# Another program order for a fused polysketch-attention and feed-forward kernel

## Chip, cores and metric

The kernel runs on one core of a Trainium2 chip. The metric is the device time of one execution in microseconds (us); the figure for a kernel is the median over its runs. The core has five engines that run side by side, each through its own instruction queue and strictly in the order in which the instructions stand there: TensorE (PE, matrix products; its weight loads are shown apart as PEld), VectorE (DVE), ScalarE (ACT), GpSimd (POOL) and SyncE (SP, which here only issues DMA transfers). Matrix products write to PSUM; everything else lives in SBUF. Engines wait for one another through semaphores.

## What is computed

Two stages: attention with a quadratic feature map (4 batches, 4 heads, 1088 positions, head dimension 32, r = 8), whose output is laid out as 4352 tokens by 128 and goes through a multiplicative feed-forward network.

```python
def phi(x):                                       # attention, r = 8
    a = np.einsum('rd,bhsd->bhsr', S1, x)
    b = np.einsum('rd,bhsd->bhsr', S2, x)
    return np.einsum('bhsi,bhsj->bhsij', a, b).reshape(*x.shape[:-1], r * r)
q_p, k_p = (phi(q), phi(k))
kv = np.einsum('bhsf,bhsd->bhfd', k_p, v)
z = np.sum(k_p, axis=2)
num = np.einsum('bhsf,bhfd->bhsd', q_p, kv)
den = np.einsum('bhsf,bhf->bhs', q_p, z)[..., None] + 1e-06
attn_out = num / den
x = attn_out.transpose(0, 2, 1, 3).reshape(4352, 128)
a = x @ w1                                        # feed-forward: 128 -> 1024
b = x @ w2
h = a * b @ w3                                    # 1024 x 1024
out = h @ w_out                                   # 1024 -> 128
```

q, k and v are float32; the sketch matrices S1, S2 and the four weights arrive as float64 and are read as raw 64-bit words.

## The kernel before

The whole program is a set of some 950 named steps, each a few instructions, that the function `make_steps` defines, and one long string `ORDER` that names every step once. The entry function runs the steps in the order of the string and then chains the instructions of each engine, so that the place of a name in `ORDER` is the place of its instructions in its engine's queue. Nothing else schedules; buffers are handed out in that order too, and a step that takes a buffer waits until the earlier users of that buffer are done.

The names have two parts, the object and the step.

**Weights, `w0` to `w10`.** `w0` and `w1` hold halves of w1 and w2, `w2` holds w_out, `w3` to `w10` the eight row blocks of w3. Each is 1 MB of 64-bit words. `.load` issues the DMA (SP, L291 to L301; there are three buffers `raw`), `.c` and `.m` read the high and the low words (ACT, L184 and L321), `.j` and `.a` put them together (DVE, L332 and L337).

**Folds, `f0` to `f7`.** Because h is used only through w_out, the kernel computes w3 @ w_out once: `.t` transposes a block of w3 (DVE, L365), `.m` multiplies it with w_out (16 products on PE, L371), `.o` copies the result out (ACT, L375).

**Keys, `k0` to `k3` (one per batch).** `.load`, `.loadr`, `kh.load` and `v.load` are DMAs; k, v and kh have a single buffer each, so batch b + 1 can be loaded only when batch b's readers are done. `.max`, `.g`, `.lead`, `.rest` split k into an exact leading part and a rest (DVE); `.gram0` and up multiply k by itself (PE, L480, 144 small products for a batch), which leads through `.Gm`, `.Gt`, `.Ga`, `.Gb`, `.T0`, `.T1`, `.Ta`, `.Tb`, `.Ts`, `.N0`, `.N1`, `.Na`, `.Nb`, `.Nh`, `.Nf`, `.Nl` to the matrix with which a query's denominator is found. `.kT`, `.ab`, `.abt`, `.kp` form the key features, `.kv` (64 small products) and `.kvr` multiply them by v, `.kvm`, `.kzt`, `.kz` bring the result into the form the queries need. `kr0` and `kr1` do the same for the last 64 positions of two batches. For `k0` the feature product `.kp` runs on POOL (L503).

**Queries, `q0` to `q7` and `qr`** (512 tokens each, `qr` the 256 that remain). `.tr`, `.max`, `.l2`, `.l1`, `.rm` transpose and split (DVE and ACT), `.A0`, `.C0` are the small products with the sketch and with N (PE, L798 to L887), a dozen short DVE steps from `.sm` to `.rc` give the denominator, `.phi` the features, `.pt0`, `.pt1` and `.x` bring them through PE (L1008, L1053), `.xT` is the copy of the 128 x 512 block of x (ACT). `q0` has further steps `.A1`, `.C1`, `.xs`, `.xt` of the same kind.

**Feed-forward, `g0` to `g7` and `gr`,** over the same token blocks. For each of the eight column blocks c: `.ca` is x @ w1 (PE, L1087), `.cc` copies it out of PSUM (ACT, L1092), `.cb` is x @ w2 (PE, L1097), `.cm` multiplies the two (DVE, L1103, into one of 17 buffers `ab`), `.co` adds the product with the folded weights into the output (PE, L1109). `g0.1a` is thus the first product of column block 1 of token block 0. `.oT` transposes the output (DVE), `.st` stores it (SP, L1065). The products `.ca`, `.cb` and the folds share three PSUM buffers `h`. The two instructions of such a step take 0.86 us.

**Warm-up, `warm0` to `warm8`:** products of zeros (L176; 15, 5, 3, 1, 6, 15, 4, 2 and 5 of them) that nobody reads. `c.act` is a dummy copy that makes ACT load its function table.

A weight load and its product are called a pair below; the program has 2134 pairs on PE.

Of the kernel before, what the change touches and what calls it, by code (L numbers as in the profile page):

```python
# [30 lines left out]


ORDER = """
c.zeros v0.zero c.ident c.mask k0.zero k0.load0 k0.loadr k0.load1 s.load c.act q0.load v0.loadr w0.load
k0.max0 w1.load k0.max1 k0.nat1 kr0.load warm0 k0.tr1 k0.g0 k0.g1 k0.lead0 k0.kT1 k0.lead1 kh1.load k0.nat0
k0.rest0 s.words k0.rest1 warm1 k0.gram0 s.pair q0.tr s.split k0.gram1 q1.tr w0.c v0.load q0.max k0.tr0
k0.Gm s.T k0.Gt k0.kT0 w0.j k1.zero s.P k1.load q0.l2 s.blk k0.Ga s.blkh warm2 k0.ab1 k0.Gb q0.l1 s.Pp k1.loadr
q0.A0 k0.ab0 w2.load q0.rm k0.T0 k0.T1 k0.abc0 kr0.tr k0.abc1 k0.Ta k0.kp0 warm3 q0.C0 w1.c k1.kT1 q1.max w1.m
k0.Tb q0.sma q0.restT kr0.kT k0.Ts w0.m k0.kp1 warm4 k0.kv0 k1.max k0.N0 k0.N1 q0.sta w3.load k0.Na q0.sha
k0.Nh k0.Nb q0.sla kr1.load warm5 q0.A1 k0.Nl k0.Nf kr0.ab q0.sca k0.kv3 q0.smy kr0.abc q0.al k0.kv1 kr0.kp  # L40
q0.sty q0.C1 q0.phi w4.load q1.l2 k0.kv2 k0.kvr v1.zero q1.l1 q0.shy warm6 q0.pt0 k0.kvm q0.C1t q0.sly k0.kzt
q0.pt1 q0.pc0 q0.scy v1.load q0.p01 q1.A0 k0.kz q0.pc1 q0.p2 warm7 q0.x q1.rm q0.p12 w1.j w3.c q0.dn q0.de w2.c
q1.sm q1.C0 q0.rc q1.st q0.xs w0.a q0.xt q0.xT q1.sh w2.m k1.g w1.a warm8 g0.1a g0.1b w2.j g0.1c w5.load 
k1.lead g0.0a g0.1m kr1.tr g0.6a kr1.kT g0.0c k1.rest g0.0b w2.a kr1.ab g0.6b g0.6c w3.m g0.5a g0.0m g0.6m
g0.7a g0.5c w6.load q1.sl kr1.abc k1.kT0 g0.5b w3.j g0.7b g0.5m q1.load w4.c k1.gram0 w3.a g0.7c k1.ab w4.m
q1.sca q1.scy f0.t k1.gram1 w5.c w7.load k1.gram2 q1.al q1.p01 g0.2a q1.p2 k2.zero g0.7m q1.p12 kh2.load
g0.4a w4.j g0.2c q1.dn f0.m g0.4c w4.a w6.c k2.load q1.de k1.Gm f1.t v1.loadr w5.m g0.2b g0.4b q1.rc g0.2m f0.o
w10.load f1.m k1.Gt q1.bs q2.tr w6.m q1.phi g0.0o k1.abt f1.o w8.load q1.pt1 k1.Ga q2.max q1.pt0 w5.j
g0.3a q1.pc0 g0.4m q1.pc1 k2.loadr q1.x k1.kp1 g0.1o q1.xT w5.a q2.l2 g1.1a g0.3c k1.Gb g0.3b f2.t g1.1c q2.l1
k1.T0 k1.T1 g1.5a g0.3m f2.m k1.Ta g1.5c k1.kp0 w7.c w7.m w6.j g1.1b k1.Tb g1.6a w6.a f2.o w9.load k1.kv0  # L50
g1.1m k1.kv2 k1.kv3 k1.kv1 w8.c w7.j k1.kvr g0.2o f3.t g1.5b w7.a f3.m g1.6c k1.kvm k1.Ts g1.5m w8.j g1.6b
f3.o f4.t k1.N0 w9.c k1.N1 g1.4a g1.6m g1.4b k1.Na g1.4c k2.max f4.m g1.4m w8.m k1.Nb g1.0a k2.g w9.j f4.o
g1.0b k1.Nf q2.rm g1.0c w10.c k2.lead g0.3o k1.Nl k1.Nh g1.3a g1.0m k2.rest g1.2a g1.3c w9.m g0.4o q3.tr w8.a
k2.gram0 k2.gram1 k2.kT1 q2.C0 f5.t k2.kT0 k2.gram2 q3.max q2.A0 k2.ab k3.zero k3.loadr v2.zero w9.a kr1.kp
q3.l2 v2.load f5.m g1.2c q2.At q3.l1 q2.Ct q2.sm q3.rm g1.7a f5.o q2.st f6.t g1.3b w10.m g0.5o q2.sh w10.j
f6.m q2.sl g1.3m q2.sca q2.scy q2.al q3.A0 q2.p01 f6.o q3.C0 g1.7c w10.a g1.2b q2.p2 f7.t g1.7b q2.p12 q2.dn
f7.m k2.Gm q2.de q1.restT q2.rc q2.load q2.bs q3.At v2.loadr q3.Ct g0.6o kh3.load q2.phi f7.o g0.7o k2.abt
q2.pt0 k3.load g0.oT q2.pt1 g1.2m k1.kzt g1.0o g0.st k1.kz q2.pc0 q3.sm g1.7m q2.pc1 g1.2o k2.Gt q3.st g1.5o
q3.sh q3.sl q2.x k2.kp0 g1.3o q2.xT q3.sca k3.max g2.7a g2.1a k3.g k2.Ga q3.p01 k2.kp1 g2.7b g2.1c g2.7c g1.1o
q5.tr g1.6o q5.max q3.al k3.lead g1.4o q4.tr g1.7o k2.Gb g2.5a g2.7m q4.max g2.1b q3.scy k3.rest g2.5b k2.kv0  # L60
q3.p2 k3.gram0 g2.1m q3.p12 g2.5c k3.gram1 k3.kT0 g2.5m k2.kv3 k2.kv1 k2.kv2 g1.oT k2.kvr k3.gram2 v3.zero
v3.load k2.kvm q3.dn k2.T0 k2.T1 g2.2a k3.Gm k2.Ta g2.3a k2.Tb v3.loadr g2.2c k2.Ts q3.de q4.l2 g1.st q3.rc
k2.N0 q3.bs k2.N1 q3.phi g2.2b q4.l1 g2.3c g2.0a g2.2m k2.Na g2.3b g2.0c k2.Nb q3.pt1 k2.Nh k3.kT1 g2.0b g2.3m
q3.pt0 q4.rm g2.6a k2.Nf g2.0m g2.4b g2.6c k3.Gt k2.Nl q3.pc0 g2.4a q3.pc1 q3.x q4.A0 q3.xT q4.C0 g2.4c k3.ab
g2.0o k3.abt g2.4m g3.3a g2.6b g2.2o g2.6m k3.Ga g3.3b q4.At g3.3c q4.sm g2.5o q4.st q4.Ct g3.2b g3.3m q4.sh
g3.2a k3.kp0 k2.kzt g2.1o g3.2c q5.l2 g3.2m g3.4a k3.kp1 g2.4o g3.4c k2.kz q4.sl q5.l1 g3.4b q4.sca k3.Gb g3.6a
# [12 lines left out]
g5.5c q6.bs g5.6a g4.oT g5.6b g4.st g5.6c qr.xT g5.0o g5.6m q7.sm g5.5b q7.st g5.4a g5.5m q7.sh g5.4b g5.4c
q6.phi g5.5o q7.Ct g5.1a g5.4m q6.pt0 g5.3b q6.pc0 q6.pt1 g5.3a q6.pc1 g5.1c q6.x g5.3c g5.3m g5.1b q6.xT g5.6o  # L80
g5.1m q7.sl g5.4o q7.sca g5.1o g5.3o g6.1a g5.2o g6.1c g6.1b g6.4a g6.1m q7.scy g6.6a q7.al g6.4c q7.p01 g6.4b
g6.6c g5.7o g6.4m q7.p2 g6.6b g5.oT q7.p12 g6.0a g5.st g6.6m q7.dn g6.0b g6.0c g6.5a g6.0m g6.3a g6.5c g6.3b
g6.3c g6.5b g6.3m q7.de gr.2b g6.5m g6.0o q7.rc q7.bs g6.2a q7.phi gr.2a g6.2c g6.4o gr.2c gr.2m g6.6o g6.2b
gr.0a g6.2m q7.pt1 gr.0b gr.0c q7.pt0 gr.0m g6.7a q7.pc0 g6.7b g6.7c q7.pc1 q7.x g6.7m g6.5o q7.xT g7.1a g7.1b
g7.1c g7.0a g7.1m g6.2o g7.3a g6.3o g7.3c g7.0c g7.0b g6.1o g7.0m g6.7o g7.3b g6.oT g7.4a g6.st g7.3m g7.4b
g7.4c g7.2b g7.4m g7.2a g7.6a g7.2c g7.2m g7.0o g7.6c g7.2o g7.5a g7.1o g7.5c g7.6b g7.7a g7.6m g7.5b g7.7c
gr.5a g7.5m g7.7b gr.6a g7.7m g7.5o gr.6c gr.5c g7.3o gr.6b gr.5b g7.6o gr.5m gr.6m gr.4b gr.4a g7.4o gr.4c
gr.4m gr.1b gr.1a g7.7o gr.1c gr.1m gr.3a g7.oT gr.3b gr.3c gr.7a g7.st gr.3m gr.0o gr.7c gr.6o gr.2o gr.5o
gr.7b gr.3o gr.7m gr.1o gr.4o gr.7o gr.oc gr.ot gr.oT gr.st
"""  # L90


# [4 lines left out]
def make_steps(ctx, tc, q, k, v, S1, S2, moe_w1, moe_w2, moe_w3, moe_w_out, out):  # L97
    nc = tc.nc
    dve, act, pe, pool, sp = nc.vector, nc.scalar, nc.tensor, nc.gpsimd, nc.sync
# [398 lines left out]
    def kv(b):  # L498
        a = acc[b]
        f = {}  # L500
# [5 lines left out]
        if b == 0:  # L506
            for half in range(2):
# [22 lines left out]

                @step(f"k{b}.abc{half}")
# [609 lines left out]
    for g in range(8):  # L1141
        b, half = divmod(g, 2)
# [56 lines left out]
```

## Time and profile before

| what | value |
|---|---|
| time, median of 3 runs | 279.46 us (279.44 to 281.6) |
| span of the profiled execution, first to last instruction | 278.9 us |
| PE busy | 263.7 us, 95% of the span |
| DVE busy | 187.6 us, 67% |
| ACT busy | 97.1 us, 35% |
| POOL busy | 8.2 us, 3% |
| first feed-forward product `g0.1a` starts | 36.60 us |
| last product of `gr` ends | 274.06 us |

The profile shows one execution: busy time of each engine, the chain of work that ended last followed back from the end, groups of instructions by line, who waited for whom, and every engine's instructions in order of time. Times inside it count from the first instruction. The profiled span lies 0.56 us under the median.

### The profile page before, as it was taken

The page shows a single profiled execution, that of the slowest core. Times are in us where ns is not written, and L with a number is a line of the kernel's source. Part 1 is how long each engine was busy: PE and PEld are TensorE (multiplying, and loading weights), DVE is VectorE, ACT ScalarE, POOL GpSimd, SP SyncE. Part 2 cuts the span into 40 slices and gives each one's busy share as a digit, 9 for nine tenths or more (in the row PEclk, how much of TensorE's full clock was granted, in tenths as well). Part 3 has the DMA queues.
Part 4 walks back from the last instruction along what each step waited for, and adds up shares of the span by engine and source line. Part 5 has one row for each costly group of instructions (what it writes and reads, how often), then busy time and mean ns, then how long its engine had stood idle before and what let it go on. Part 6 is the DMA issues. An engine that isn't in the chain of part 4 may idle for free.

```text
span 278.9 us, 5282 instructions
## 1 busy us (share of the span) xinstructions
PE 263.7 (95%) x2134; PEld 149.7 (54%) x2134; DVE 187.6 (67%) x427; ACT 97.1 (35%) x167; POOL 8.2 (3%) x33
## 2 busy tenths in 40 slices
PE   7985999799998999979999999999999999999993
PEld 5874956455656763454544545445544446344572
DVE  4978699798999988976398855466773255231330
ACT  3552466636273213123231143163223221413121
POOL 2051000000001000000000000000000000000000
PEclk9998699999999999999999999999999999999999
DMA  7999969999800364040002200200020020002011
GB/s 201 329 250 217 211 130 213 237 235 213 166 1 6 79 170 105 0 112 10 2 0 81 38 2 0 38 2 0 2 39 0 1 40 0 0 5 33 0 20 39
DMA packets 32168, 22.50 MB, mean 81 GB/s; under 512 B 21392, under 2 KB 26640, under 8 KB 32144
## 3 DMA queue, kind: packets, MB, share of 16 engines
q1 hardware_dynamic: 31600, 21.64, 35.2%
q10 hardware_dynamic: 544, 0.52, 0.6%
q8 instruction: 17, 0.28, 0.5%
q14 instruction: 7, 0.06, 0.1%
HBM read 19.93 MB, written 2.23 MB: 79 GB/s over the span
## 4 chain that ended last, share of the span: by engine, by line
PE 85%; DMA 6%; SPq 2%; issue 2%; DVE 1%; ACT 1%; ACTq 0%; DVEq 0%
PE a_ps L1087 21%; PE b_ps L1097 21%; PE ps_o L1109 20%; PE ps_w3o L371 5%; DMA raw<-in_moe_w_dram 3%; PE ps_x L1053 3%; PE ps_ph L1008 3%; PE ps_c L798 3%; DMA k<-in_k_dram 3%; PE ps_g L480 2%; PE ps_kv L578 1%; PE ps_ab L553 1%; PE ps_xt L1027 1%; SPq L1065 1%; DMA out_dram<-oT 1%
## 5 line engine op out<-in xcount | busy, mean ns | idle before, releaser
L1103 DVE TENSOR_TENSOR ab<-ffa,b_ps 128x512 f32<-128x512 f32 (+1 forms) x72 | 46.8, 651 | 57.8 <-PE b_ps L1097 44.3
L1092 ACT COPY ffa<-a_ps 128x512 f32<-128x512 f32 (+1 forms) x72 | 39.7, 562 | 101.6 <-PE a_ps L1087 89.7
L1087 PE MATMUL a_ps<-xT,w 128*128 128x512 f32 (+1 forms) x144 | 69.1, 575 | 0.1
L1097 PE MATMUL b_ps<-xT,w 128*128 128x512 f32 (+1 forms) x144 | 68.8, 572 | 0.0
L1109 PE MATMUL ps_o<-ab,w3o 128*128 128x512 f32 (+1 forms) x144 | 67.4, 574 | 0.0
L1097 PEld LDWEIGHTS b_ps<-xT,w 128*128 128x128 f32 x144 | 26.4, 190 | 28.4 <-issue 25.2
L1109 PEld LDWEIGHTS ps_o<-ab,w3o 128*128 128x128 f32 x144 | 26.1, 190 | 26.2 <-issue 23.1
L1087 PEld LDWEIGHTS a_ps<-xT,w 128*128 128x128 f32 x144 | 25.9, 190 | 25.8 <-issue 20.7
L371 PEld LDWEIGHTS ps_w3o<-wo,w3T 128*128 128x128 f32 x128 | 15.5, 192 | 5.9 <-issue 5.0
L371 PE MATMUL ps_w3o<-wo,w3T 128*128 128x128 f32 x128 | 16.1, 277 | 1.7 <-issue 1.7
L184 ACT ACTIVATE cv_c<-raw 128x1024 f32<-128x1024 f32 x11 | 12.7, 1166 | 8.9 <-DMA raw<-in_moe_w_dram 8.9
L1014 ACT COPY pT<-ps_ph 128x512 f32<-128x512 f32 (+1 forms) x18 | 9.9, 566 | 10.9 <-PE ps_ph L1008 10.9
L321 ACT ACTIVATE cv_m<-raw 128x1024 int32<-128x1024 uint32 x11 | 12.7, 1156 | 0.0
L1008 PEld LDWEIGHTS ps_ph<-ident,ph 128*128 128x128 f32 x68 | 9.1, 151 | 6.6 <-issue 4.6
L176 PE MATMUL idle_ps<-zeros 128*128 128x256 bf16 x56 | 10.6, 340 | 1.7 <-DVE zeros L151 1.1
L480 PE MATMUL ps_g<-kk 128*32 128x64 f32 x288 | 10.4, 228 | 1.7 <-issue 1.7
L480 PE MATMUL ps_g<-k,kk 128*32 128x32 f32 x288 | 9.9, 197 | 1.3 <-issue 1.3
L1008 PE MATMUL ps_ph<-ident,ph 128*128 128x128 f32 x68 | 11.0, 290 | 0.0
L480 PEld LDWEIGHTS ps_g<-kk 128*32 128x32 f32 x288 | 8.8, 112 | 3.5 <-issue 2.1
L480 PEld LDWEIGHTS ps_g<-k,kk 128*32 128x32 f32 x288 | 9.2, 114 | 1.8 <-issue 1.8
L365 DVE STREAM_TRANSPOSE w3T<-w3c 128x1024 f32<-128x1024 f32 x8 | 9.8, 1230 | 0.0
L337 DVE CUSTOM_DVE_ANT_0 w3c<-w3c,cv_m 128x2048 uint16<-128x2048 uint16 x8 | 9.6, 1203 | 0.0
(196 smaller groups left out, 281.4 us busy)
## 6 DMA issues: line engine op xcount, KB each, us to landing
raw<-in_moe_w_dram SPq DMA_DIRECT2D x32, 256.0 KB, 7.8
qh<-in_q_dram SPq DMA_DIRECT2D x4, 544.0 KB, 4.2
raw<-in_moe_w_dram SPq DMA_DIRECT2D x4, 512.0 KB, 6.1
out_dram<-oT SPq DMA_DIRECT2D x32, 64.0 KB, 2.0
kh<-in_k_dram SPq DMA_DIRECT2D x12, 128.0 KB, 7.5
k<-in_k_dram SPq DMA_DIRECT2D x3, 512.0 KB, 7.5
v<-in_v_dram SPq DMA_DIRECT2D x12, 128.0 KB, 3.3
raw<-in_moe_w_out_dram SPq DMA_DIRECT2D x4, 256.0 KB, 9.2
```

The lines of the kernel that those rows point to most:

```text
L176: pe.matmul(t[:, :256], zeros[:, :128], zeros, start=True, stop=True)
L184: act.activation(dst, hi.bitcast(F32), ACT.Prelu, scale=2.0 ** -112, alpha=-2.0 ** 32)
L321: act.mul(shape(x["m"], 1, True), words(0).bitcast(U32), 2.0 ** -29)
L371: pe.matmul(t["o"], w3T[ko][:, c], wo[:, c], start=c == 0, stop=c == NC - 1)
L480: pe.matmul(o[h * D:(h + 1) * D], lhs, rhs, start=start, stop=stop, skip_group_check=True)
L1008: pe.transpose(t[:, j * 128:(j + 1) * 128], ph_cols(j, p), ident)
L1014: act.copy(s["pT"][:, p, :n], s["pp", p][:, :n])
L1087: pe.matmul(x["a"][:, :w], w_of(0, c), xT[g][:, c0:c0 + w], start=True, stop=True)
L1092: act.copy(x["s"][:, :w], x["a"][:, :w])
L1097: pe.matmul(x["b"][:, :w], w_of(1, c), xT[g][:, c0:c0 + w], start=True, stop=True)
L1103: dve.tensor_mul(ab_sb[g, c][:, c0:c0 + w], x["s"][:, :w], x["b"][:, :w])
L1109: pe.matmul(o_ps[g][:, :n], w3o[:, c], ab_sb.pop((g, c))[:, :n], start=c == 0, stop=c == NC - 1)
```

## The change

The string `ORDER` is replaced by another permutation of the same step names; every step and every instruction stays. A second edit goes with it: the dictionary that holds the transposed keys `kT` is indexed by batch and half in place of half alone, so that the steps `.kT` of one batch may stand ahead of readers of another. The three products of `warm2` now come last of all, after the final store, and `c.act` stands far down, so that ACT's table load goes with its first real copy, `k0.nat0`.

The diff, cut to the start of the string, the stretches around the key products of batches 1 to 3, and the end:

```diff
-c.zeros v0.zero c.ident c.mask k0.zero k0.load0 k0.loadr k0.load1 s.load c.act q0.load v0.loadr w0.load
-k0.max0 w1.load k0.max1 k0.nat1 kr0.load warm0 k0.tr1 k0.g0 k0.g1 k0.lead0 k0.kT1 k0.lead1 kh1.load k0.nat0
-k0.rest0 s.words k0.rest1 warm1 k0.gram0 s.pair q0.tr s.split k0.gram1 q1.tr w0.c v0.load q0.max k0.tr0
-k0.Gm s.T k0.Gt k0.kT0 w0.j k1.zero s.P k1.load q0.l2 s.blk k0.Ga s.blkh warm2 k0.ab1 k0.Gb q0.l1 s.Pp k1.loadr
-q0.A0 k0.ab0 w2.load q0.rm k0.T0 k0.T1 k0.abc0 kr0.tr k0.abc1 k0.Ta k0.kp0 warm3 q0.C0 w1.c k1.kT1 q1.max w1.m
-k0.Tb q0.sma q0.restT kr0.kT k0.Ts w0.m k0.kp1 warm4 k0.kv0 k1.max k0.N0 k0.N1 q0.sta w3.load k0.Na q0.sha
...
-q1.sm q1.C0 q0.rc q1.st q0.xs w0.a q0.xt q0.xT q1.sh w2.m k1.g w1.a warm8 g0.1a g0.1b w2.j g0.1c w5.load 
...
-g0.7a g0.5c w6.load q1.sl kr1.abc k1.kT0 g0.5b w3.j g0.7b g0.5m q1.load w4.c k1.gram0 w3.a g0.7c k1.ab w4.m
-q1.sca q1.scy f0.t k1.gram1 w5.c w7.load k1.gram2 q1.al q1.p01 g0.2a q1.p2 k2.zero g0.7m q1.p12 kh2.load
...
-k2.gram0 k2.gram1 k2.kT1 q2.C0 f5.t k2.kT0 k2.gram2 q3.max q2.A0 k2.ab k3.zero k3.loadr v2.zero w9.a kr1.kp
...
-q5.tr g1.6o q5.max q3.al k3.lead g1.4o q4.tr g1.7o k2.Gb g2.5a g2.7m q4.max g2.1b q3.scy k3.rest g2.5b k2.kv0
-q3.p2 k3.gram0 g2.1m q3.p12 g2.5c k3.gram1 k3.kT0 g2.5m k2.kv3 k2.kv1 k2.kv2 g1.oT k2.kvr k3.gram2 v3.zero
...
-gr.7b gr.3o gr.7m gr.1o gr.4o gr.7o gr.oc gr.ot gr.oT gr.st
+k0.zero c.zeros warm7 c.mask k0.loadr warm5 v0.zero k0.load0 k0.max0 c.ident k0.load1 s.load k0.nat0 k0.g0 k0.lead0
+k0.nat1 w0.load q0.load kr0.load k0.max1 s.words warm8 warm3 w0.c k0.tr0 k0.rest0 k0.tr1 k0.gram0 k0.g1 k0.lead1
+s.pair k0.rest1 k0.gram1 k1.zero s.split q0.tr k0.kT1 k0.kT0 s.T s.blkh q0.max s.P warm6 q0.l2 kr0.tr k0.Gm q1.tr
+k0.Gt s.blk k0.ab1 w1.load k1.loadr k0.Ga w0.j q0.l1 q0.A0 q0.rm s.Pp k0.Gb warm1 v0.loadr k0.ab0 k0.T0 q1.max
+k0.T1 w0.m k0.Ta k0.Tb q0.C0 k1.load k0.N0 k1.max q0.sma k0.Ts k0.N1 q0.sta k0.abc1 v0.load k0.kp1 k1.g kr0.kT
+k0.Na k0.abc0 k0.Nb k0.kp0 k0.kv0 k0.Nh q0.sha k0.kv3 k0.kv1 kr0.ab k0.Nf q0.A1 k0.Nl q0.sla q0.sca q0.smy w1.m
+q0.al q0.phi kr0.abc w3.load q0.sty k0.kv2 q0.shy q0.C1 q0.C1t kr0.kp warm0 q0.sly q0.pt0 k0.kvr k1.lead k0.kvm
+q0.scy q0.p01 q0.p2 q0.pt1 k0.kzt q1.l2 q1.l1 q1.A0 q1.sm q0.p12 q0.dn q0.pc0 q1.rm q0.de q0.pc1 k0.kz w3.c q0.x
+kh1.load k1.kT0 q0.rc q1.C0 w1.c w1.j q0.xs q1.st w0.a q0.xt w1.a q0.xT warm4 q1.sh g0.1a g0.1c k1.rest q1.sl
+kr1.load g0.0b g0.0a w3.m g0.0c w4.load w4.c kr1.tr w3.j g0.6a w2.load g0.1b k1.gram0 q1.sca k1.gram1 w3.a q1.scy
+g0.1m q1.al g0.0m kr1.kT k1.gram2 k1.kT1 q1.p01 q1.p2 g0.6b w2.m k1.Gm g0.6c q1.p12 q1.dn w4.m k1.Gt k2.zero g0.5a
...
+g1.0b g0.3o w8.a k2.rest g1.0m kh3.load w9.m w10.c k2.gram0 k2.gram1 w10.m q3.max k2.ab f5.t kr1.kp q2.sm w10.j
...
+q3.C0 q2.sca g1.3m q2.al f7.t q2.p01 q2.scy q2.p2 k2.gram2 k2.Gm k3.zero k3.loadr q2.p12 k2.abt q2.dn k3.load q3.At
...
+g2.2a k2.kv0 k2.kv3 q4.max q3.bs q3.phi k2.kv1 k2.kv2 k3.gram0 k2.kvr k2.kvm k3.gram1 k2.T0 k2.T1 g2.2c q4.l2 g2.3a
+g2.2m k2.Ta k2.Tb g2.3c q4.l1 k2.Ts g1.2o k2.N0 k2.N1 g2.6a g2.0a g2.3b g2.6c v3.zero k2.Na k2.Nf k2.Nh g2.3m k2.Nb
...
+k3.kT1 q3.load q4.A0 k3.gram2 g2.0m q4.C0 q4.At q4.sm q4.st g1.oT k3.ab g2.0o q4.Ct q4.sh g2.4m g3.2a q4.sl q5.l2
...
+gr.oc gr.ot gr.oT gr.st warm2
...
-                    kT[half] = sb("t2", [128, 512], name="kT")
-                    act.copy(kT[half], f["pt", half].rearrange("p j x -> p (j x)"))
+                    kT[b, half] = sb("t2", [128, 512], name="kT")
+                    act.copy(kT[b, half], f["pt", half].rearrange("p j x -> p (j x)"))
```

## The prediction

> **What bounds the kernel now.** First the page: how full the engines are, and where.
>
> ```profile
> PE 263.7 (95%) x2134; PEld 149.7 (54%) x2134; DVE 187.6 (67%) x427; ACT 97.1 (35%) x167; POOL 8.2 (3%) x33
> PE   7985999799998999979999999999999999999993
> DVE  4978699798999988976398855466773255231330
> PEclk9998699999999999999999999999999999999999
> DMA  7999969999800364040002200200020020002011
> q8 instruction: 17, 0.28, 0.5%
> ```
>
> PE is full from about slice 6 on, but for dips. VectorE is as full up to slice 17 (some 120 us) and half idle after, so it may bound the first part, never the second. The DMA engines are full up to 75 us. Next the chain of waits in order of time (start, length, what), as its head and its breaks:
>
> ```profile
> 14.23 7.41 DMA k<-in_k_dram
> 21.76 1.35 DVE k_g L140
> 31.22 2.46 PE ps_xt L1027 x16
> 36.60 1.12 PE a_ps L1087 x2
> ...
> 51.40 1.72 issue
> ...
> 87.41 1.25 issue
> ...
> 120.21 1.73 issue
> ```
>
> Up to 36.60 no feed-forward product can run: the chain goes through the load of `k1`, VectorE's `k1.max`, the denominator steps and `q0`. From 36.60 the chain is PE, but for three breaks in which PE waits for nothing that the profile shows. Last, cumulative windows (length; busy and count of PE, PEld, DVE, ACT, POOL; clock, DMA) up to those breaks:
>
> ```profile
> 0.00:51.41 51.41, 45.31 (x602) 34.22 (x602) 41.75 (x106) 26.34 (x41) 6.94 (x29) 0.93 0.96 224
> 0.00:87.30 87.30, 79.48 (x982) 55.46 (x983) 74.25 (x165) 44.39 (x67) 6.94 (x29) 0.96 0.86 192
> 0.00:120.20 120.20, 111.13 (x1363) 74.49 (x1364) 105.18 (x227) 52.05 (x82) 8.17 (x33) 0.97 0.71 160
> ```
>
> The breaks come after 602, 982 and 1363 pairs: 380 and 381 apart, three times 127. The instruction queue moved 17 blocks of 16 KB, one per 2134/17 = 126 pairs. I read the breaks as PE at the end of a block with the next not there.
>
> **Term 1, the start.** Before, `k1.load` was issued at 13.80, behind `kh1.load` and `v0.load`; it landed at 21.6, `k1.max` ran 21.76 to 23.1, `k0.Nh` ended at 24.16, `q0.xs` began at 33.72, `g0.1a` at 36.60. In the new order `k1.load` stands ahead of `kh1`, `v0` and `w3`. It still waits for the last reader of the single k buffer, `k0.gram1`. ACT's table load (1.28 us, before under the k load) now comes behind that load, so `k0.nat0` ends near 6.4 and the transposes of `k0.nat0` and `nat1` (1.5 us) stand ahead of the gram products (3.7 us): gram ends near 11.5, against 11.2 before. `k1.loadr` and `v0.loadr` (0.6 each) go first, so `k1.load` starts near 13.3. Landing: 2.0 us (shortest median of a bulk row, the stores) to 7.4 (its own row), that is 15.3 to 20.7. VectorE meanwhile: `s.split` to 10.5, `q0.tr` 0.6, `s.blkh` after PE's transposes at 12.2, then `q0.max`, `q1.tr`, `w0.j`, `q0.rm` (0.6 each), `s.Pp` 1.3, the `k0.G`, `Ta`, `Tb` steps: `k1.max` at 18.6 at the earliest. From there to `Nh` are 3.4 us of rows: 22.1 with the data early; with `k1` at 20.7, 23.8. `Nh` to `xs` was 9.56 us with 2.0 us of idle for `q0.x` (PE at clock 0.5 after a 2.72 us gap); the steps now listed there (`k1.lead`, `k1.kT0`, `q1.rm`, `w1.j` among them) sum to 9.2: `xs` 31.2 to 33.0; then `xs`, `xt`, `xT` 2.0 to 2.9. `g0.1a`: 33.2 to 35.9. Costs not seen before on this path: VectorE's `T_p` step took 1.74 us in place of 0.18 while POOL ran `kp`; that can now hit a step that matters, so 36.6 is the other end. I take 34.2, nearer the early end because `k1` no longer shares with `kh1`: **-2.4 us (-3.4 to 0).** The 56 warm-up products (0.12 to 0.23 us each) are redistributed in gaps; the last three run under the final store (2.1 us): 0.
>
> **Term 2, the breaks.** The 857th pair came at 85.10 and the 984th at 88.67; the 1238th at 118.44 and the 1365th at 121.95: 3.5 us for a block is what the fetch allows with DMA quiet. The 476th to 603rd took 6.8 us under full DMA (46.31 to 53.13). Now PE's work per block, from rows (0.86 us per feed-forward step, 1.78 a fold, 0.6 per 48 gram pairs, 0.22 per 16 kv pairs, 0.97 `C0`, 0.86 `k.ab`). Before, the three broken blocks hold 4.9, 2.1 and 1.7 us: `k1`'s gram with `k1.ab`; `k2`'s with `q2.C0`; `k2`'s kv with `k3`'s gram. All others hold 9.5 or more. In the new order `k1.ab` stands 9 products after the gram, `k2.gram2` and `k3.gram2` are split off from their batch, `q2.C0` comes four products ahead. The same boundaries then cut blocks of 11.5, 15.1, 13.3, 5.5, 6.4, 18.1, 10.7, 7.9 us and longer. None is under 3.5. At the price of full DMA two would break for 1.7 us together, but DMA is quiet after 75 us. **-4.7 us (-4.7 to -3.0; 0 if the reading is wrong).**
>
> [...]
>
> **Term 3, VectorE as the next bound.** What is late once PE comes earlier? From `g0.1a` on, PE's work is the same to 0.2 us (225.8 against 225.6 by rows; spent 237.5, so 4.7 in breaks and 7.2 in small turns between kinds). I sum VectorE's steps from `q0.xs` and PE's from `g0.1a` to each point where PE needs VectorE. Before, VectorE is at most 1.4 us behind PE's bare sum. In the new order it is behind from `k2.gram0` on, by 2.5 at `f6.m`, most at `k2.N0`: VectorE 82.5 us from the end of `xs` (32.9 when `g0.1a` is at 34.2), thus 115.4 bare; PE 78.4 bare and 3.9 of turns, 116.5. VectorE's idle time between 35 and 120 was 6.0 us:
>
> ```profile
> 50.00:55.00 5.00, 3.28 (x20) 2.37 (x19) 3.46 (x7) 3.61 (x6) 0.00 (x0) 1.00 1.05 242
> 80.00:85.00 5.00, 5.00 (x50) 2.21 (x52) 5.00 (x10) 3.28 (x4) 0.00 (x0) 1.00 0.00 2
> 85.00:90.00 5.00, 3.75 (x187) 3.25 (x174) 5.00 (x8) 1.49 (x3) 0.69 (x3) 1.00 0.03 7
> 100.00:105.00 5.00, 5.00 (x29) 3.45 (x28) 3.91 (x7) 1.15 (x4) 0.00 (x0) 1.00 0.94 254
> ```
>
> Its largest piece, 1.54 us, lies beside the break at 51.4. With half of the idle, 3.0, it reaches `k2.N0` at 118.5: **+2.0 us (0 with none, +5.0 with all).** The weights are not behind this: `w7` to `w10` are now loaded in a row; by the bytes ahead of them (213 GB/s) they land at about 60 to 79, VectorE wants them from 67 to 83. `w2` moves behind `w3`, `kh1`, `kr1`, `w4` and lands near 39; its ACT step stands ahead of `g0.6c` and can hold that copy by about 1 us, which the gram products on PE cover. After `k2.N0` VectorE has slack and the rest is PE: 147.4 and 3.2 of turns.
>
> **The end** is the same: the last output copy needs both PE's last product (274.06) and the store before it (274.14); `g7.st` now has 6 us of products behind `g7.7o` where it had 5. 4.84 us, 0.
>
> **Sum** against the execution's own 278.9: -2.4 - 4.7 + 2.0 + 0.2 = 274.0; the median lies 0.56 above: **274.6 us.**
>
> **Rivals.**
> - *VectorE keeps up* and the start is at its early end: -3.4 - 4.7 + 0.2 gives 271.6. For it: VectorE's idle lay partly beside PE's breaks. Against: VectorE stands at 5.00 of 5 us from 80 to 95.
> - *The gain ends in a wait for VectorE:* all 6.0 us of idle stay. `k2.N0` at 32.9 + 82.5 + 6.0 = 121.4, plus 150.6 + 4.84 + 0.56: 277.4, and 278.8 with a start gained by 1.0 only. No measurable change (one per cent, 2.8 us, is what a measurement tells from none).
> - *Slower, VectorE's in-order queue:* its steps up to `k2.N0` have no slack now, so each wait put on it by another order of copies and products is paid in full. With twice the idle, 12 us: 127.4, so 283.4. It turns slower than before from 8.1 us of idle on, and measurably from 10.9. For it: 98% busy leaves no room, and the new order has not been lived in by this engine; against: no wait that I could place by sums exceeds 3 us.
> - *The breaks are something else* and stay: 274.6 + 4.7 = 279.3, less VectorE's waits, which they would cover (2.0): 277.3. No change.
>
> **Numbers.** Forecast 0.50 (its own range 272.5 to 276.6), VectorE keeps up 0.15, gain ends in a wait 0.14, breaks stay 0.07, slower 0.14. Faster by over 1% (under 276.7): 0.65; within: 0.21; slower: 0.14. Range 270.8 to 280.5: the lower end takes in the early start with a little less turning, the upper both cases of no change and the beginning of the slow one.
>
> **What would show it.** `g0.1a` near 34 (33.2 to 36.6); `k1.max` without a wait for DMA over 2 us; no PE wait on "issue" over 1 us after it, 127 pairs never passing under 3.5 us; `k2.N0` near 118 with PE waiting for VectorE about 2 us in all between 70 and 118; the end of PE 151 us later. Wrong if `k2.N0` comes after 124, if breaks of 1.2 us or more appear at other multiples of 127 pairs, or if the stretch after 120 has PE gaps, for which I found no reason.

## The result and the profile after

| | before | changed |
|---|---|---|
| median (range, runs) | 279.46 us (277.37 to 283.24, 19) | 276.66 us (274.96 to 277.55, 19) |
| ratio | | 0.9893, 95% interval 0.9868 to 0.9918 |
| profiled execution: time, span | | 277.46, 275.7 us |
| `g0.1a` starts | 36.60 | 36.79 |
| `k2.N0` starts | 124.33 | 120.56 |
| last product of `gr` ends | 274.06 | 270.91 |

(The ratio leaves out the disturbed runs, which the medians and ranges include, so the two can differ a little.) The change is faster by 1.1%. That is 2.8 us where 4.9 were forecast: 276.66 us lies within the range of 270.8 to 280.5, and 0.06 us above the narrower 272.5 to 276.6 that the forecast gave itself. The page of the changed kernel, busy times and slices:

```profile
PE 266.5 (97%) x2134; PEld 150.8 (55%) x2134; DVE 189.2 (69%) x427; ACT 97.6 (35%) x167; POOL 8.3 (3%) x33
PE   7899999989999999999999999999999999999994
DVE  4888899998899999957988456666682534223130
PEclk9965899999999999999999999999999999999999
DMA  6989479999951075200410002001020002001020
q8 instruction: 17, 0.28, 0.5%
```

From the tenth slice on PE never drops under 9 until the last: the three dips are gone, with the same 17 blocks fetched. New is the 6 and 5 in PEclk, in the slices from 14 to 28 us. The chain of waits (start, length, what):

```profile
8.07 3.17 PE ps_g L478 x141
...
26.89 2.82 PE idle_ps L174 x15
29.71 0.44 PE ps_ph L1006 x4
30.14 0.29 PE ps_kv L583 x8
...
30.46 0.29 DVE kvm L589
...
34.50 0.68 DVE xs L1031
...
53.72 0.97 issue
...
58.82 1.27 PE ps_w3o L369 x9
```

The load of `k1` is no longer in it, nor is an "issue" of PE; the one at 53.72 lies between two steps of VectorE, with VectorE (`q1.phi`) and PE both busy beside it. In its place stand PE's small products and `warm0`, most of them at half clock, and behind them VectorE up to 58.8. The chain goes through VectorE again between 77.8 and 92.2 and between 113.3 and 118.7, but there PE waits for it only twice, 0.2 us each. By stages (length; busy and count of PE, PEld, DVE, ACT, POOL; clock, DMA share, GB/s):

```profile
5.20:15.40 10.20, 8.02 (x186) 6.84 (x186) 8.84 (x27) 6.74 (x11) 0.20 (x1) 1.00 0.83 258
15.40:29.10 13.70, 13.70 (x138) 11.81 (x135) 11.78 (x38) 3.82 (x8) 4.53 (x3) 0.50 1.02 248
29.10:36.79 7.69, 7.05 (x69) 6.24 (x67) 6.61 (x17) 4.01 (x6) 0.00 (x0) 1.00 0.46 108
36.79:120.56 83.77, 82.55 (x937) 48.56 (x937) 80.43 (x157) 39.32 (x61) 1.62 (x6) 1.00 0.65 146
35.00:60.00 25.00, 24.12 (x247) 13.84 (x247) 24.88 (x43) 16.27 (x23) 0.40 (x2) 1.00 0.93 215
```

The same view of the kernel before, around its own stretch of half clock:

```profile
22.40:25.80 3.40, 1.26 (x51) 1.20 (x54) 3.30 (x17) 0.21 (x1) 0.40 (x1) 1.00 1.12 216
25.80:32.60 6.80, 6.18 (x63) 5.34 (x56) 5.43 (x16) 3.74 (x6) 0.42 (x2) 0.50 1.07 209
```

So before, PE ran at half clock for 6.8 us, now for 13.7, and `g0.1a` starts no earlier. The gain came after it: to the end of PE 237.5 us before, 234.1 now. VectorE is busy 24.88 of the 25 us from 35 on. The changed kernel's 19 times lie in two groups that go with the mean clock listed with each run: ten of 276.66 to 277.55 us with a clock of 0.971 to 0.975 and nine of 274.96 to 276.14 with 0.978 to 0.990. In the profiled runs a mean clock of 0.974 went with 13.7 us at half speed (the changed kernel) and one of 0.986 with 6.8 (`e12_m_first` below).

### The profile page after: what moved, and what is told of

The parts are those of the page before. It is cut to its first block, busy times and chain, and to the rows that moved or that the text cites. A ratio compares the mean times of both kernels' runs of the same rounds, so it can differ in the third digit from the quotient of the medians.

```text
span 275.7 us, 5281 instructions
## 1 busy us (share of the span) xinstructions
PE 266.5 (97%) x2134; PEld 150.8 (55%) x2134; DVE 189.2 (69%) x427; ACT 97.6 (35%) x167; POOL 8.3 (3%) x33
## 4 chain that ended last, share of the span: by engine, by line
PE 78%; DVE 17%; issue 2%; DMA 1%; ACT 1%; ACTq 0%; DVEq 0%
PE ps_o L1107 20%; PE a_ps L1085 18%; PE b_ps L1095 18%; PE ps_w3o L369 3%; PE ps_x L1051 3%; DVE ab L1101 2%; PE ps_c L796 2%; PE ps_ph L1006 2%; DVE w3c L335 2%; DVE w3T L363 2%; PE ps_g L478 2%; PE ps_kv L576 1%; PE idle_ps L174 1%; DMA k<-in_k_dram 1%; DVE kp L501 1%
## 5 line engine op out<-in xcount | busy, mean ns | idle before, releaser
L1006 PEld LDWEIGHTS ps_ph<-ident,ph 128*128 128x128 f32 x68 | 8.2, 140 | 7.0 <-issue 5.1
L1006 PE MATMUL ps_ph<-ident,ph 128*128 128x128 f32 x68 | 10.1, 273 | 0.0
L478 PE MATMUL ps_g<-kk 128*32 128x64 f32 x288 | 9.2, 224 | 0.0
L995 DVE TENSOR_TENSOR ph<-s_al,s_bs 128x1024 f32<-128x1024 f32 (+1 forms) x8 | 9.1, 1136 | 0.1
L174 PEld LDWEIGHTS <-zeros 128*128 128x128 bf16 x56 | 6.6, 124 | 4.3 <-issue 1.2
```

The costliest lines, as they stand in the source:

```text
L174: pe.matmul(t[:, :256], zeros[:, :128], zeros, start=True, stop=True)
L478: pe.matmul(o[h * D:(h + 1) * D], lhs, rhs, start=start, stop=stop, skip_group_check=True)
L1006: pe.transpose(t[:, j * 128:(j + 1) * 128], ph_cols(j, p), ident)
```

## Experiments

Two theories of the breaks (instruction fetch or something else), two of the start (halves of the order are independent, or not), then the clock, VectorE and PE's gap. Zero products that nobody reads are added in some; nothing else is changed but the order, except where said.

**One half of the order alone.** `e1_start_before` has the old order of all steps up to `g0.1a` and the rest in the new order, `e2_start_after` the reverse; the few steps that this would drop (`k1.lead` and `k1.kT0` in the first) stand just ahead of `g0.1a`. The diff of the first against the changed kernel, cut to its first line:

```diff
-k0.zero c.zeros warm7 c.mask k0.loadr warm5 v0.zero k0.load0 k0.max0 c.ident k0.load1 s.load k0.nat0 k0.g0 k0.lead0
...
+c.zeros v0.zero c.ident c.mask k0.zero k0.load0 k0.loadr k0.load1 s.load c.act q0.load v0.loadr w0.load k0.max0
...
```

> Old order up to the first feed-forward product g0.1a, the new order for all that follows. My theory: the start is worth nothing by itself (g0.1a came at 36.79 against 36.60), the whole gain lies behind it, in the breaks of PE that are gone: g0.1a near 36.6, no PE gap over 1 us named issue after it, k2.N0 near 120.5, span 275 to 276.5, about 1.1% faster than before. Rival: the new start prepares what the new rest needs (k1.lead, k1.kT0, w1.j done earlier), and the rest loses with the old start: k2.N0 after 122 and span over 277.5.

> The other half: new order up to g0.1a, the old order for all that follows. My theory: g0.1a near 36.8, the three breaks are back at the pairs 603, 984 and 1365 (1.2 to 1.9 us each, 4.7 in all), span 278 to 279.5, within 0.4% of before. Rival: the start carries the gain in a way that its end does not show (VectorE further ahead): span under 277.

Measured: `e1_start_before` 279.70 us (276.43 to 283.35, 10 runs), ratio to before 0.9978 (0.9924 to 1.0032); `e2_start_after` 283.41 (281.54 to 284.65, 4), ratio 1.0141 (1.0062 to 1.0220). Neither half is a gain by itself in the median. In `e1_start_before` the signs of the rival came (`k2.N0` at 122.51, a span of 277.6 us), though three of its ten runs took 276.43 to 276.92. What PE waited for between 40 and 130 us in `e2_start_after` (us in total, times, longest):

```profile
PE ps_w3o L371 <- issue: 3.6, 1, 3.6
PE ps_g L480 <- issue: 2.5, 2, 1.4
```

Its breaks stand at pairs 601, 982 and 1363 as before, after 127 pairs in 3.4 and 3.2 us for the last two: they go with the second half of the order. The first one took 3.57 us, and behind it the clock was halved for another 3.4 us (56.5 to 59.9). In `e1_start_before` there is no such break in that window, but one gap of PE, where VectorE (start, length, line, step) does this:

```profile
52.81 1.21 DVE L503 TENSOR_TENSOR kp<-kabt 128x1024 f32<-128x1024 f32 x1
53.94 1.23 DVE L365 STREAM_TRANSPOSE w3T<-w3c 128x1024 f32<-128x1024 f32 x1
55.10 1.18 DVE L503 TENSOR_TENSOR kp<-kabt 128x1024 f32<-128x1024 f32 x1
56.20 0.68 DVE L1103 TENSOR_TENSOR ab<-ffa,b_ps 128x512 f32<-128x512 f32 x1
```

These are `k1.kp0`, `f1.t`, `k1.kp1` and only then `g0.3m`, which frees the PSUM buffer for PE's next product. PE waits 2.83 us for it (54.10 to 56.93), and the clock is halved from 57.7 to 61.1. The changed kernel has the same queue, with a wait of 0.81 us at 58.01. `g0.1a` came at 35.10 in `e1_start_before`, without half clock ahead of it, in steps that needed 36.60 in the profiled run of before.

**Moving the block borders.** Small zero products (32 columns) shift every later pair within its block of instructions: 96 in the kernel before behind `warm4`, 48 in the changed kernel behind `warm6`.

```diff
             t = ps(tag, [128, 512], "idle_ps")
+            for _ in range(96 if name == "warm4" else 0):
+                pe.matmul(t[:32, :32], zeros[:, :32], zeros[:, :32], start=True, stop=True)
```

> The kernel before with 96 small extra products of zeros (32 columns, nobody reads them) behind warm4, in the 2.7 us in which PE waits for VectorE at 22 us. They shift every later pair by 96 places against the blocks of 127. My theory (a break comes where a block of 127 pairs is run through in under 3.5 us): with the boundaries shifted the blocks hold 13.4, 9.2, 13.2, 12.0, 2.8, 16.5, 11.3, 5.0 us of work, so two of the three breaks vanish and one of under 1 us stays, at the 1111th pair of the new count, inside the batch-2 gram: 3 to 4 us faster than before, unless the start is later by what the products take (at most 1 us). Rival: the breaks belong to the steps where they stood (a wait that the profile does not name): they stay in f0.m, k2.gram2 and k3.gram2, 4.7 us in all, time the same or slower.

> The changed kernel with 48 small extra products of zeros behind warm6, in the 1.3 us in which PE waits at 13 us. My theory: the boundaries now cut out blocks of 1.6 us (to the 603rd pair, in the batch-1 gram, near 42 us) and 1.7 us (to the 1365th, batch 2's kv and batch 3's gram, near 113 us): two breaks of 1.2 to 1.9 us each come back in a kernel that had none over 1 us; time 0 to 3 us longer than the changed kernel, since VectorE is late beside both. Rival (breaks belong to steps): no break; time the same. A second thing may show: with the gap at 13 us filled PE may hold the full clock after 15.4 us, and then the start is earlier by up to 2 us.

Measured: `e3_before_96` 278.04 us (277.08 to 280.14, 10), ratio 0.9955 (0.9919 to 0.9990), faster with 96 products more. The three breaks are gone, and the small one that was expected at pair 1111 did not come: a wait for VectorE falls into its block. What PE still waits for between 40 and 130 us:

```profile
PE ps_ab L555 <- DVE kT L548: 1.0, 1, 1.0
PE a_ps L1089 <- ACT ffa L1094: 0.4, 1, 0.4
PE ps_g L482 <- DVE kk L474: 0.4, 1, 0.4
PE ps_T L666 <- DVE kvm L593: 0.3, 1, 0.3
PE ps_w3o L373 <- DVE ab L1105: 0.2, 1, 0.2
```

The largest, 0.99 us at pair 1095, ends when VectorE has transposed `kT` (86.60 to 87.27). In the kernel before PE has no such wait there: the breaks had covered them. So from `g0.1a` to `k2.N0` the kernel takes 85.39 us for 87.73, 2.3 us less and not 4.7, and the median gains 1.4 where 3 to 4 were expected.

`e4_after_48` took 285.95 us (283.19 to 287.20, 4), ratio 1.0232 (1.0155 to 1.0310): 9.3 us above the changed kernel, for 48 products that lie between 11.9 and 15.3 us. From its chain of waits:

```profile
44.53 2.89 issue
...
125.14 1.33 issue
```

The breaks came at the forecast pairs 602 and 1363. In windows, the first and the stretch from it on:

```profile
44.53:47.42 2.89, 0.00 (x1) 0.00 (x1) 1.20 (x4) 0.91 (x1) 0.00 (x0) 0.90 1.05 218
46.80:53.70 6.90, 6.28 (x11) 2.91 (x12) 3.66 (x9) 0.59 (x1) 0.40 (x2) 0.51 1.01 226
```

A third break lies ahead of them and was not expected: at pair 223 PE stands still for 1.83 us (13.03 to 14.86) in the midst of the 48 zero products, which have no data to wait for. `g0.1a` came at 38.11, 1.3 later. The two later breaks are 4.2 us together. From 46.85 on, just before the end of the first of these, the clock is halved for 6.8 us, and PE, busy for 6.28 of the 6.90 us shown, loses about half of that. Together that is 8.6 us, where the two profiled spans differ by 8.3 and the medians by 9.3.

That the instructions were late can be read from the traces themselves, which hold the packets of the instruction queue, 17 of 16 KB in each profile. Some of them, beside the breaks:

| kernel, pairs before the break | PE stands still (us) | instruction packet (us) | from the packet's end to PE's next product |
|---|---|---|---|
| before, 602 | 51.40 to 53.13 | 50.49 to 51.51 | 1.62 |
| before, 982 | 87.41 to 88.67 | 86.48 to 87.41 | 1.25 |
| before, 1363 | 120.21 to 121.94 | 119.22 to 120.69 | 1.25 |
| `e2_start_after`, 601 | 52.06 to 55.63 | 52.94 to 53.97 | 1.66 |
| `e4_after_48`, 223 | 13.03 to 14.86 | 12.32 to 13.41 | 1.45 |

The fourteen profiles have eleven gaps of PE over 0.4 us that no wait explains. All stand at pairs 223, 349, 601 or 602, 982 and 1363, that is at steps of 127 to within three pairs (349 is a break of 0.62 us in the kernel before and of 1.41 in `e1_start_before`, both among zero products), and in all of them PE goes on 1.25 to 1.66 us after the end of a packet. At the other 213 block borders PE comes to the new block some 2 us or more after the packet's end, and does not stand still. So breaks appear and vanish with the count of pairs, in two kernels in which no other work was moved, and each ends shortly behind a fetch: the reading as instruction fetch holds.

**Warm-up products.** `e5_no_warm0` puts the 15 products of `warm0` (26.89 in the chain above) behind everything; `e9_start3` does so too, issues `q0.load` ahead of `w0.load` and moves `k0.ab0` behind `k0.T1`.

```diff
-q0.al q0.phi kr0.abc w3.load q0.sty k0.kv2 q0.shy q0.C1 q0.C1t kr0.kp warm0 q0.sly q0.pt0 k0.kvr k1.lead k0.kvm
+q0.al q0.phi kr0.abc w3.load q0.sty k0.kv2 q0.shy q0.C1 q0.C1t kr0.kp q0.sly q0.pt0 k0.kvr k1.lead k0.kvm
...
-gr.oc gr.ot gr.oT gr.st warm2
+gr.oc gr.ot gr.oT gr.st warm2 warm0
```

> The changed kernel with the 15 zero products of warm0 moved from in front of q0.pt0 to the very end. In the changed kernel they ran 26.82 to 29.54 us at half clock while q0.phi was done at 27.6, so q0.pt0, k0.kvr and k0.kvm came about 1.9 us late, and VectorE idled 1.05 us for k0.kvm. Theory A (they sit on the path of the start): q0.pt0 near 27.8, VectorE's idle before k0.kvm gone, g0.1a 35.5 to 36 in place of 36.79, and since VectorE sets the pace behind it the time falls by 0.5 to 1.1 us. Theory B (they keep PE's clock up): the half clock lasts longer than 13.7 us from 15.4 and reaches the feed-forward products; time the same or up to 3 us longer.

> The changed kernel with three steps of the start moved: warm0 to the end as above, q0.load ahead of w0.load (VectorE waited 1.19 us for q), k0.ab0 behind k0.T1 so that the second k0.kp on POOL starts after VectorE's T_p step, which took 1.56 us beside it. Theory (the start lost its gain to these three): T_p near 0.2 us, k1.max near 19 in place of 20.95, g0.1a 34 to 35.5, time 1 to 2.5 us shorter than the changed kernel if VectorE, which sets the pace up to 60 us, is earlier by as much. Rival (the start is bound by PE at half clock, q0.C0 in front of k0.N0): g0.1a within 0.7 us of the run without warm0 alone.

Measured: 280.74 us (276.43 to 282.77, 10), ratio 0.9969 (0.9912 to 1.0027), and 281.15 (277.32 to 282.74, 10), ratio 0.9973 (0.9928 to 1.0018): the whole gain of the change is lost. The windows of `e5_no_warm0`:

```profile
14.60:28.20 13.60, 12.64 (x132) 11.01 (x130) 11.63 (x38) 3.91 (x8) 4.53 (x3) 0.50 0.91 234
28.20:41.90 13.70, 13.29 (x63) 11.23 (x63) 10.64 (x22) 4.31 (x7) 0.00 (x0) 0.50 0.54 120
```

The clock stays halved for 27.3 us, until the first feed-forward products have run, and `g0.1a` comes at 39.61 (38.92 in `e9_start3`). Nor is that one run alone: nine of the ten runs have a mean clock of 0.963 or less, where none of the 31 of the changed kernel (with those of `e16_after_again` below) is under 0.968. `warm0` takes 2.8 us of PE on the chain, and without it `g0.1a` comes 2.8 us later.

`e9_start3` shows the two other moves as well. With POOL's second `kp` behind it, VectorE's `T_p` step took 0.18 us and `k1.max` began at 18.70, as expected (in `e5_no_warm0` 1.56 us and 20.30). But VectorE then waited 1.57 us for the products of `q0.C0`, which PE ran at half clock, and `k0.N0` began at 21.51, against 21.46 in `e5_no_warm0`. `g0.1a` is 0.69 us earlier, which is what the rival said: here PE at half clock bounds the start.

**Less work for VectorE.** `e10_less_dve` leaves out the steps `w3.a` to `w10.a`, so the low words of w3 are not added: VectorE is busy 71.85 us between `g0.1a` and `k2.N0` in place of 80.43.

```diff
+            if n > 2:
+                return
             d = x["d"].bitcast(I32)
```

> The changed kernel without the steps w3.a to w10.a: the low words of w3 are not added in, 9 us of VectorE work less between 40 and 90 us, nothing else left out. Theory (VectorE is the bound between g0.1a and k2.N0, at a price of about 1.5 us over PE's own turns): no wait of PE for VectorE there, k2.N0 near 119 in place of 120.56, time 1 to 2 us shorter. Rival (PE's loss is its own turns and buffers): k2.N0 within 0.5 us of 120.5, time the same. A loss of over 2 us would mean that VectorE cost more than my sum says.

Measured: 275.62 us (274.78 to 276.68, 4), ratio 0.9835 (0.9784 to 0.9887). `g0.1a` to `k2.N0` took 82.99 us where the changed kernel took 83.77. 8.6 us less of VectorE's work are worth 0.8; a gap of PE of 0.64 us for `g0.3m` near 58 is still there. With `k2.N0` at 119.79 that lies between the two theories.

**One step ahead of the key products.** `e12_m_first` moves `g0.3m` ahead of `k1.kp0`, nothing else; `e15_m_first_again` is the same kernel again, `e16_after_again` the changed kernel again, on one chip.

```diff
-k1.abt kh2.load q1.phi f0.m q1.pt0 w5.c k1.kp0 f0.o g0.2b f1.t k1.kp1 g0.0o q1.pt1 w6.m g0.3m q1.pc0 q1.pc1 f1.m
+k1.abt kh2.load q1.phi f0.m q1.pt0 w5.c g0.3m k1.kp0 f0.o g0.2b f1.t k1.kp1 g0.0o q1.pt1 w6.m q1.pc0 q1.pc1 f1.m
```

> The changed kernel with the one step g0.3m moved ahead of k1.kp0, f1.t and k1.kp1 on VectorE (3.4 us of work in front of which PE waits with a full set of PSUM buffers: 0.81 us at 58 us in the changed kernel, 2.83 us in the run with the old start, where PE's clock fell to half for 3.4 us after it). Theory: no PE gap over 0.4 us between 50 and 60; 0 to 0.8 us shorter in a run like the profiled one. It tells what the run-to-run spread is worth too: if the gap sometimes grows over 2.5 us the spread of this kernel's runs shrinks.

> The same kernel as e12, again and in more rounds, next to the changed kernel itself (e16). If g0.3m ahead of the key products is a gain by itself, its median is 274.4 to 275.0 us, 1.5 to 2.5 us under that of e16. If e12 was only lucky with the clock in its four runs, it comes out within 0.7 us of e16.

> The changed kernel again, for the direct comparison with e15 on one chip: 275.0 to 277.5 us, median near 276.7. If the two groups of its times (near 275.5 and near 277.0 us) come from one window of lowered clock of 6.8 us or two, the granted clock listed with the runs is about 0.985 in the short runs and 0.973 in the long ones.

Measured: `e12_m_first` 274.58 us (274.40 to 274.88, 4), ratio to before 0.9797 (0.9763 to 0.9832); `e15_m_first_again` 274.97 (274.22 to 275.68, 6), ratio 0.9870 (0.9820 to 0.9919); `e16_after_again` 276.92 (274.63 to 279.37, 12), ratio 0.9908 (0.9871 to 0.9946). On the last chip the medians differ by 1.95 us, as expected, though the two intervals overlap; the traces tell the two kernels apart. All that PE waited for in `e12_m_first` from 40 to 130 us:

```profile
PE ps_T L664 <- DVE kvm L591: 0.2, 1, 0.2
PE ps_w3o L371 <- DVE w3T L365: 0.2, 1, 0.2
```

and its windows:

```profile
19.30:26.10 6.80, 5.20 (x92) 4.26 (x93) 6.06 (x22) 0.88 (x2) 0.80 (x2) 0.50 1.05 227
50.00:60.00 10.00, 10.00 (x55) 6.56 (x54) 9.96 (x13) 6.19 (x10) 0.00 (x0) 1.00 0.90 210
34.77:117.46 82.69, 82.29 (x937) 48.55 (x937) 80.10 (x157) 39.32 (x61) 1.62 (x6) 1.00 0.66 148
```

PE is busy 10.00 of the 10 us around the moved step. From `g0.1a` to `k2.N0` it took 82.69 us, and 82.67 to 82.69 in the three other profiles with the move, against 83.77 and 83.75 in the two without it. That 1.1 us is the gain of the move. The rest of the difference goes with the clock: in these two profiles it was halved for 6.8 us, with `g0.1a` at 34.77 and 34.79, in `e16_after_again` for 13.7 with 36.28, although the order up to there is the same. In `e16_after_again` the runs with a mean clock of 0.972 to 0.975 took 276.65 to 277.53 us, those with 0.984 to 0.990 took 274.63 to 275.73: the two groups, with two runs beside them.

**Filling PE's gap near 13 us.** Both start from `e12_m_first`. `e13_m_first_gap` makes `warm6` 14 products long in place of 4; `e14_m_first_q0` issues `q0.load` ahead of `w0.load`, so that VectorE need not wait for `q0`'s data.

```diff
-WARM = [15, 5, 3, 1, 6, 15, 4, 2, 5]
+WARM = [15, 5, 3, 1, 6, 15, 14, 2, 5]
```

```diff
-k0.nat1 w0.load q0.load kr0.load
+k0.nat1 q0.load w0.load kr0.load
```

> The changed kernel with g0.3m ahead of k1.kp0 (as in e12), and warm6 with 14 zero products of 256 columns in place of 4: ten more of them fill the gap of 1.3 us that TensorE has near 13 us. Theory A: the lowered clock that began at 15.4 us in the changed kernel and at 19.3 us in e12 is set off by that gap; then the clock stays full at least until 19 us, the first feed-forward product starts at 34.8 us or earlier in every run, and the median is 273.5 to 274.5 us, with runs closer together. Theory B: when the lowered clock falls is not set by this gap; then its start lies anywhere from 14 to 26 us as in the kernels so far, and the median is that of e15 within 0.5 us, or some 0.5 us above it for the ten pairs more.

> As e12, and q0.load issued ahead of w0.load, so that VectorE doesn't wait 1.2 us for the data of q0.tr and TensorE's gap near 13 us falls to some 0.4 us. Theory A (that wait delays the start): the first feed-forward product starts 0.5 to 1.2 us earlier than in e15 at an equal length of lowered clock, the median is 273.4 to 274.1 us. Theory B (VectorE has room to catch up, or w0, which now lands later, makes VectorE wait at w0.j): no gain, 274.4 to 275.5 us.

Measured: `e13_m_first_gap` 274.47 us (273.96 to 275.51, 6), ratio 0.9851 (0.9806 to 0.9895); `e14_m_first_q0` 275.54 (274.66 to 275.90, 6), ratio 0.9878 (0.9834 to 0.9922). Windows of `e13_m_first_gap`:

```profile
5.40:22.50 17.10, 14.02 (x256) 12.07 (x258) 15.28 (x45) 8.25 (x15) 4.06 (x3) 1.00 0.95 269
22.50:25.90 3.40, 3.40 (x80) 2.69 (x69) 3.23 (x13) 0.87 (x2) 0.63 (x1) 0.50 0.80 188
```

and of `e14_m_first_q0`:

```profile
4.60:14.80 10.20, 8.62 (x184) 6.84 (x182) 8.72 (x27) 6.20 (x11) 0.20 (x1) 1.00 0.84 265
14.80:28.50 13.70, 13.67 (x137) 11.84 (x138) 12.14 (x38) 4.48 (x8) 4.53 (x3) 0.50 1.03 239
```

With ten more zero products on the whole 128 x 128 array the clock held until 22.5 us, `g0.1a` came at 34.59, and none of the six runs had a mean clock under 0.986; of `e15_m_first_again` two in six had, of `e14_m_first_q0` four in six. But in `e14_m_first_q0` PE had no gap over 0.4 us from 6.8 to 30.8 us, and the clock fell at 14.8 all the same. So it does not take that gap to set it off; what does is not shown. The runs of 0.986 of `e14_m_first_q0` and `e15_m_first_again` take the same (274.66 and 274.68; 274.22 to 275.03): VectorE's wait for `q0` costs nothing here, so theory B of that run holds. Six runs are few to say how often the long stretch comes.

## Why the prediction was right, and where not

**Term 1, the start, failed: 0.19 us later in place of 2.4 earlier.** The sum priced the products of the start at the clock of the profiled run of before, and put VectorE's long `T_p` step at nothing. The mechanism was there: `k1.load` was no longer waited for, `k1.max` ran without idle time at 20.95 (forecast 18.6 to 20.7), and with the clock halved for 6.8 us, as in the profiled run of before, the same order reached `g0.1a` at 34.77 and 34.79 (forecast 34.2). That is -1.8 of the -2.4. The late `k1.max` is the step that I had named as a cost that can hit. The steps on VectorE and POOL around it in the changed kernel:

```profile
18.60 1.95 POOL L501 TENSOR_TENSOR kp<-kab 128x1024 f32<-128x1024 f32 x1 [0.56 <-ACT kab L532]
19.03 1.56 DVE L135 SCALAR_TENSOR_TENSOR T_p<-T_g,T_t 32x32 f32<-32x32 f32 x1
20.63 0.18 DVE L679 TENSOR_TENSOR T_p<-ps_T,T_p 32x32 f32<-32x32 f32 x1
20.95 1.35 DVE L138 TENSOR_REDUCE k_g<-k 128x1 f32<-128x1152 f32 x1
```

The 32 x 32 step took 1.56 us beside POOL's `kp` (1.93 and 1.96 in `e13_m_first_gap` and `e12_m_first`) where a step of its size takes 0.18, and `k1.max` stands behind it. I listed this as a reason for the range's end of 36.6 and gave it nothing in the value. In `e12_m_first` the step stands on the chain of waits (17.55, 1.97 us), so it can be the missing 0.6 us. Where `q0.C0` runs at half clock, as in the changed kernel, it is not on the chain, and `e9_start3` gained nothing at `k0.N0` by taking it out. That share of 0.6 us is not shown. The other 2.0 us (34.77 to 36.79) are the longer stretch of half clock, 13.7 us for 6.8. The small products of `q0.C0`, `k0.kv` and `q0.C1` ran at half speed, and `warm0`'s 15 products (2.82 us in the chain) held `q0.pt0`. The sum took the clock of the profiled run as given and looked only for waits. Where the clock falls changes from run to run, and the new order has it lowered for longer in most runs: a mean clock of 0.990 or more was listed for 22 of 55 runs of the kernel before (on three chips) and for 2 of 31 of the changed one.

**Term 2, the breaks, held: none is left, -4.7 us.** The order cut the blocks as worked out; the shortest after 80 us took 5.25 us (forecast 5.5). `e3_before_96` and `e4_after_48` show that the count of pairs places them, and the packets that they end with the fetch. Three corrections: 127 pairs were also passed in 3.14 us (`e4_after_48`) and 3.18 (`e2_start_after`), so the floor of 3.5 us is nearer 3.1. A break of 2.9 us or more went with 3.4 or 6.8 us at half clock in both runs that had one, a cost that the sum did not have. And the term is not a gain by itself: taken out of the old order the breaks were worth 2.3 us (`e3_before_96`), since waits for other engines took their place; in the new order the stretch from `g0.1a` to `k2.N0` is 4.0 us shorter (83.77 for 87.73). Of the 224 block borders in the fourteen profiles PE passed 213 without a break; the three that follow short blocks in the kernel before cost 4.7 us.

**Term 3, VectorE as the next bound, held with a smaller price: 1.1 us for 2.0.** `g0.1a` to `k2.N0` was forecast as 78.4 bare, 3.9 of turns and 2.0 of VectorE, 84.3 in all, and took 83.77. `e12_m_first` splits it: with no wait for VectorE over 0.2 us left it took 82.69, so turns were 4.3 and VectorE 1.1 (0.81 of it is PE's wait at 58.01). I had it too wide: the sum let VectorE's idle time in total set the delay, and put the wait between 70 and 118. `e10_less_dve` shows that the total counts little (8.6 us less, 0.8 us gained), and the trace that the one wait lies at 58: PE needed one product, `g0.3m`, that stood behind three longer steps. What cost was the order within VectorE's queue at one place.

**The rest held.** `k2.N0` came at 120.56, which is 118.0 (forecast 118.5) with the start's 2.6 us taken off; from there to PE's end it took 150.35 us (forecast 150.6) without a gap; the end took its 4.8. Of the rivals, the slower one did not come, and "the breaks are something else" fell to the two kernels with shifted blocks. Against the forecast span of 274.0 the profiled one has +2.6 from the start, -0.5 up to `k2.N0` and -0.3 after it: 275.7 with the roundings. The 0.56 that I put on top joined the span of one run to the median of others. A run takes 1.8 us more than its own span (277.46 for 275.7), so by that the profiled run of before was one of some 280.7 us, above its median; the two profiled spans differ by 3.2 us, the medians by 2.8. That the total came within its range is in part luck: the start missed by 2.6 us, and the range was wide enough to hold the case of no change.

## What to carry to other kernels

Before an order is searched or edited, count what PE is given within each block of instructions, here 127 pairs. With the DMA engines quiet, blocks here that PE would pass in 1.8 to 2.3 us stalled at their end, and one that it passed in some 4 us did not (`e1_start_before`); with DMA busy, a block of 9.5 us stalled too (there, at pair 349). A handful of dummy products or another place for a batch of small ones moves or removes such a break, but look what PE will wait for once it is gone. The start full of small products had a price that went with the clock (`g0.1a` at 34.77 with 6.8 us at half clock, at 36.79 with 13.7): judge such a start over many runs and by the clock listed with each, not by one trace, and don't take dummy products on the whole array out without trying, even where they stand on the chain (without `warm0` the half clock lasted 27.3 us for 13.7). Where an engine seems full, look for the one product that another engine waits for and what stands ahead of it in the queue; moving one step gained 1.1 us, and 8.6 us less work only 0.8.

## What the runs showed of the hardware

**The granted clock fell while PE was busy too.** Stretches of half clock were 3.4 us long (`e13_m_first_gap`, and behind a gap of PE in `e1_start_before` and `e2_start_after`), 6.8 (the kernel before, `e12_m_first`), 13.7 (the changed kernel, `e14_m_first_q0`) and 27.3 (`e5_no_warm0`): one, two, four and eight times some 3.41. They began at 15.4 us in the changed kernel, at 14.8 in `e14_m_first_q0`, 19.3 in `e12_m_first`, 22.5 in `e13_m_first_gap` and 25.8 in the kernel before. The window of `e12_m_first` just before its clock falls, and one of `e13_m_first_gap` that no fall follows:

```profile
15.87:19.28 3.41, 2.97 (x25) 2.51 (x24) 3.27 (x8) 1.41 (x2) 3.41 (x2) 1.00 1.00 269
12.25:15.66 3.41, 2.94 (x30) 2.57 (x29) 3.38 (x12) 2.60 (x4) 0.00 (x0) 1.00 0.82 236
```

PE is as busy in one as in the other, 2.97 and 2.94 of 3.41 us, so its busy time does not tell them apart. The two kernels differ by ten zero products of 256 columns in `warm6`, and taking `warm0` out (`e5_no_warm0`) made the half clock longer, 27.3 us for 13.7. Whether the size of the products decides is not shown: a run with nothing but that changed was not made.

**A VectorE step of 0.18 us took as long as POOL's elementwise product had still to run:** 1.56 to 1.96 us in the thirteen profiles in which it falls beside `kp`; in the changed kernel it ended at 20.59, POOL at 20.55. In `e9_start3`, where `kp` starts after it, it took 0.18. Not every step beside `kp` was held: `T_p<-T_g,T_t`, with both inputs in SBUF, took 1.56 us, the step just before it, `T_t<-T_g,ps_T`, with one in PSUM, 0.17 beside the same `kp` (18.83 in the changed kernel). Whether the place of the inputs decides is not shown: the kernel with an input of `T_p` in PSUM was not tried.

**The breaks with the DMA engines busy varied more:** 0.62 to 3.57 us ahead of 56 us (pairs 223, 349, 601 and 602 in four kernels), 1.08 to 1.73 with them nearly quiet (pairs 982 and 1363). In these breaks the packet of the next block started 1.9 to 8.5 us after PE had come to the block before it with DMA busy, 0.6 to 1.4 us with it quiet.
